# One core, attention followed by a token- and channel-mixing block: the zero tile cleared first, tail matmul pairs put together, three element-wise steps in larger pieces

## The chip, the core and the metric

The kernel runs on one core of one Trainium2 chip. A core has a matrix engine (TensorE, PE in the profile, with its weight loads shown apart as PEld), a vector engine (VectorE, DVE), a scalar engine (ScalarE, ACT), a general engine (GpSimd, POOL) and SyncE (SP), which here only issues DMAs. Each engine works through its own queue in order. An instruction may wait for semaphores that other engines or landing DMAs raise, and everything behind it on its queue then waits too. The metric is the device time of one execution in microseconds.

## The reference

The inputs are `q`, `k`, `v` of shape (8 batches, 8 heads, 576 tokens, 64), and the weights of a mixing block over 512 channels. All of it is float32.

```python
kv  = einsum('bhsd,bhse->bhde', k, v)              # 64 x 64 per head
out = einsum('bhsd,bhde->bhse', q, kv)
out = out / sqrt(mean(out*out, -1) + 1e-6) * g_norm  # per head
x   = out.transpose(0, 2, 1, 3).reshape(8, 576, 512)
a1  = alpha1 * x + beta1
u   = x + lam * einsum('ts,bsd->btd', w_tok, a1)    # token mix, 576 x 576
a2  = alpha2 * u + beta2
y   = u + lam * (relu(a2 @ w_ch1) @ w_ch2)          # channel mix, 512 -> 2048 -> 512
```

## The kernel before

**Stages.** For each of the eight batches the kernel makes the key-value products (`kv_product`, L666), the attention output with its normalisation (`qkv_groups`, L851/L858 and the steps after them), the token mix (`tok_groups`, L1020, L1029, L1053; for batch 0 `tok_first`, L1083), a transposed and scaled copy `a2t` of the mixed rows (`ut_groups`), the first channel matmul with its ReLU (`ch1_groups`, L1169 for even and L1211 for odd batches) and the second channel matmul with the final add and the store (`ch2_groups`, L1260, L1270, L1273). Matmuls of the large stages are in bf16 with a moving operand of 512 columns (320 in odd batches).

**Tokens.** A batch's 576 tokens are four chunks of 128 and a tail of 64. The tails of two batches share one tile, so odd batches carry the tails of their even neighbour. The chunks are handled in `PAIRS = ((0, 1), (2, 3), (4,))`.

**The token mix.** For a pair of chunks the mix sums over four token chunks of 128 and the tail of 64. In batches 0 and 1 (`b < MIX`) the tail is a fifth matmul per chunk. From batch 2 on the function `group` issues for each chunk four matmuls (L1020), and then for the pair two matmuls over the 64 tail rows (L1029), one on the upper and one on the lower half of the array's rows. VectorE adds the result to `x` (L1035), then scales it by `alpha2` into `a2b` (L1041), and SyncE issues DMAs that transpose `a2b` into `a2t` (L1148). In batches 0 and 1 the transposes are matmuls against an identity (L1118), evacuated by ScalarE (L1127) or VectorE (L1128). The tails of an odd batch and of its neighbour are mixed in `tails` (L1053), one on each column half of the array.

**The start.** All weights and the first batches' inputs have to be loaded. Before the first real work and in holes of the plan TensorE gets filler matmuls on a zeroed tile `wz`, which shares its memory with `a2b` (L1572; the zeroing is L1368). VectorE clears four small tiles first (L1368 to L1371). Batch 0's mix is done in halves of 256 columns (`tok_first`, adds at L1100). Batch 1's queries are split into a high and a low bf16 part (`split_q`, casts at L533 and L534, subtractions at L621) and transposed by matmuls (L644). W_ch1 comes in four pieces and is cast to bf16 (L533, L534); W_ch2 comes in four pieces and is multiplied by `lam` into bf16 in sixteen parts of 512 columns (L1493). The third part of the parameters, `beta1` (L1299), is loaded into the first of the W_ch2 buffers once its parts have been scaled, and the loads for batch 2 stand behind it on SyncE.

**The order of the work.** The kernel first records operations with their reads and writes, and then a list scheduler (`Prog.schedule`) sets the order on every queue from priorities, assumed costs per operation and the eight PSUM banks; some operations may go to one of two engines. `Prog.plan` repeats this with priorities taken from due times of the first channel matmuls, keeps the best of eight rounds, shifts priorities at random once for each of five seeds, and schedules a last time. Where TensorE would have nothing to do before the first channel matmul, the scheduler puts in a filler. So any change of an assumed cost, a piece or a seed can move instructions on all queues. Waits on semaphores come from the recorded reads and writes. `matmul_held` (L428) issues a matmul that keeps the weights of the one before.

Of the kernel before, what the change touches and what calls it, by code (L numbers as in the profile page):

```python
# [49 lines left out]
class Prog:  # L50
# [6 lines left out]
    def __init__(self, nc, stack):  # L57
# [10 lines left out]
        self.look = 0.5  # L68

# [54 lines left out]
    def plan(self, due, rounds, seeds):  # L124
# [6 lines left out]
        def run(pri):  # L131
# [8 lines left out]
            for o in movable:  # L140
                o.pri = pri[o]
            self.schedule()
# [39 lines left out]
    def schedule(self):  # L182
# [91 lines left out]
        while left:  # L274
            progressed = False
            for e, q in queues.items():
                while q and free[e] <= t + 1e-9:
# [14 lines left out]
                    if pick is None and e == "PE" and first:  # L292

                        pick = self.op("PE", 0.43 if t < 6.0 else 0.22, lambda e: self.warm[1](e, self.warm[3]),
# [139 lines left out]
def bass_transnormer_attn__then__resmlp_affine_kernel(  # L434
# [15 lines left out]
    with ExitStack() as stack:  # L450
# [146 lines left out]
        def split_q(b):  # L597
# [3 lines left out]
            if b < 2:  # L601
                parts = [(cs, hs) for hs in HALVES for cs in PAIRS]
            else:
                parts = [(cs, ALL[0]) for cs in PAIRS]
# [406 lines left out]
        def tok_groups(b):  # L1011
            def group(cs):
                n = len(cs)
                t = P.ptile(n)
                rows = rows_of(b, cs[0])
# [9 lines left out]
                if scs < 5:  # L1025
                    def g(e):
                        for i, c in enumerate(cs):
                            r = slice(64 * i, 64 * i + 64)
                            m = e.matmul(t.ap()[:, i, :], wt[r, 4 + i, 128 * c:128 * c + 128],  # L1029
                                         rtt[r, b % 2, :], start=False, stop=True)  # L1030
                        return m
                    P.op("PE", 0.28, g, r=wtk(4) + ["wt5"] + rkeys(b, 4), w=[t])
# [7 lines left out]
                for c in cs:  # L1040
                    P.op(dve_pool(512), 0, lambda e, c=c: e.tensor_tensor(  # L1041
                        out=a2b[rows, c, :], in0=xv(b, (c,)), in1=a2_bc[rows, :], op=ALU.mult),
                        r=xkeys(b, c) + ["a2"], w=[("a2b", c)], pri=-100, port=True)
            def tails():
# [18 lines left out]
                if b > 1:  # L1063
                    P.op(dve_pool(512), 0, lambda e: e.tensor_tensor(
                        out=a2b[:, 4, :], in0=x, in1=a2_bc[:], op=ALU.mult),
                        r=xk + ["a2"], w=[("a2b", 4)], pri=-100, port=True)
            for cs in PAIRS[:2]:
                yield lambda cs=cs: group(cs)
# [3 lines left out]
        def tok_first():  # L1072

            def half(a):
                hs = HALVES[a]
                lo, hi = 256 * a, 256 * a + 256
                ts = [P.ptile(1) for g in PAIRS[:2]]

                def part(sc):
                    def f(e):  # L1080
                        for cs, t in zip(PAIRS[:2], ts):
                            for i, c in enumerate(cs):
                                m = e.matmul(t.flat()[:, 256 * i:256 * i + 256],  # L1083
                                             tok_w(sc, c), rsrc(0, sc, lo, hi),
                                             start=(sc == 0 and i == 0), stop=(sc == 4),
# [519 lines left out]
```

## Time and profile before

| what | value |
|---|---|
| median of 3 runs (lowest, highest) | 364.8 us (364.39, 364.88) |
| profiled execution, its own time | 365.61 us |
| its span, first to last instruction | 363.6 us |
| TensorE busy | 357.7 us, 98% of the span |
| VectorE busy | 240.8 us, 66% |
| ScalarE busy | 160.2 us, 44% |
| GpSimd busy | 26.6 us, 7% |
| mean DMA rate | 165 GB/s |

In the profile a row of a group reads: line, engine, operation, output<-inputs, shape, count, then busy time, mean of one in ns, idle time of the engine before them and what ended it. A timeline row reads: start in us from the span's beginning, time, engine, line, operation, output<-input, shape, count. Neighbouring matmuls overlap in these times, because a matmul's end is modelled; the pace is read from start to start. A matmul in float32 shows as two rows of the count unless it is a transpose.

### The profile page before, as it was taken

To read this page: it belongs to the slowest core of one execution; us is meant where nothing else is said; L and a number is where in the kernel's file an instruction comes from. 1 tells how busy PE (TensorE), PEld (TensorE's weight loads), DVE (VectorE), ACT (ScalarE), POOL (GpSimd) and SP (SyncE) were. 2 spreads that over 40 slices of the span, in tenths; PEclk is the share of its full clock that TensorE was granted. 3 is DMA by queue.
4 is the path that set the end of the run, shared out by engine and by line. 5 is a ranking of instruction groups with operands and counts; after the bars stand their busy time and mean duration, and the time that the engine had idled before them with its cause. 6 is when DMAs were issued, how large, how long until landed. Compare 5 with 4: busy or idle time off the path is not lost.

```text
span 363.6 us, 7716 instructions
## 1 busy us (share of the span) xinstructions
PE 357.7 (98%) x3479; PEld 203.9 (56%) x3255; DVE 240.8 (66%) x366; ACT 160.2 (44%) x277; POOL 26.6 (7%) x34
## 2 busy tenths in 40 slices
PE   7999999999999999999999999999999999999996
PEld 3788555477644654457644454457654554457644
DVE  3388997995985388866984368865986368830021
ACT  1466883248740287017740188007750186007600
POOL 4046412500000000000000000000000000000000
PEclk9999999999999999999999999999999999999999
DMA  7999928999407960299637860199027410130012
GB/s 286 367 364 382 404 112 318 374 193 274 174 21 183 286 250 1 60 159 275 237 72 187 239 241 2 43 161 260 3 58 132 132 31 0 43 117 29 2 58 87
DMA packets 79896, 60.15 MB, mean 165 GB/s; under 512 B 53037, under 2 KB 63541, under 8 KB 79736
## 3 DMA queue, kind: packets, MB, share of 16 engines
q1 hardware_dynamic: 79840, 59.67, 55.3%
q8 instruction: 26, 0.43, 0.5%
q14 instruction: 6, 0.05, 0.0%
q10 hardware_dynamic: 24, 0.01, 0.0%
HBM read 38.82 MB, written 9.44 MB: 133 GB/s over the span
## 4 chain that ended last, share of the span: by engine, by line
PE 98%; DVE 0%; issue 0%
PE ps L1260 34%; PE ps L1211 19%; PE ps L1169 14%; PE ps L1020 7%; PE ps L666 5%; PE ps L1572 2%; PE ps L851 2%; PE ps L428 2%; PE ps L1053 1%; PE ps L858 1%; PE ps L1083 1%; PE ps L1118 1%; PE ps L693 1%; PE ps L1029 1%; PE ps L1241 1%; PE ps L951 1%
## 5 line engine op out<-in xcount | busy, mean ns | idle before, releaser
L1260 PE MATMUL ps<-w,ht 128*128 128x512 bf16 x560 | 125.8, 379 | 0.0
L1158 ACT ACTIVATE ht<-ps,hb 128x512 bf16<-128x512 f32 (+1 forms) x96 | 70.9, 739 | 45.7 <-PE ps L1211 35.0
L1260 PEld LDWEIGHTS ps<-w,ht 128*128 128x128 bf16 x560 | 53.3, 98 | 62.9 <-issue 1.4
L1211 PE MATMUL ps<-a2t,w 128*128 128x320 bf16 (+1 forms) x512 | 72.4, 299 | 0.0
L1211 PEld LDWEIGHTS ps<-a2t,w 128*128 128x128 bf16 x512 | 49.4, 98 | 20.5
L1169 PE MATMUL ps<-a2t,w 128*128 128x512 bf16 x240 | 55.3, 379 | 0.8 <-issue 0.8
L728 ACT ACTIVATE kvd<-ps 64x128 bf16<-64x128 f32 x24 | 6.5, 271 | 92.3 <-PE ps L666 92.2
L1270 DVE TENSOR_TENSOR xm<-ps,xm 128x512 f32<-128x512 f32 x31 | 20.8, 685 | 28.6 <-PE ps L1260 28.5
L1169 PEld LDWEIGHTS ps<-a2t,w 128*128 128x128 bf16 x240 | 22.4, 98 | 26.4 <-issue 1.3
L890 DVE TENSOR_REDUCE small<-sq 128x16 f32<-128x1024 f32 (+2 forms) x20 | 20.5, 1026 | 16.0 <-ACT sq L888 16.0
L1020 PE MATMUL ps<-rt,wt 128*128 128x512 bf16 x112 | 26.9, 380 | 0.0
L1159 ACT ACTIVATE ht<-ps 128x512 bf16<-128x512 f32 (+1 forms) x32 | 20.2, 649 | 4.0 <-PE ps L1169 1.5
L1035 DVE TENSOR_TENSOR xm<-ps,xm 128x1024 f32<-128x1024 f32 x14 | 17.1, 1221 | 5.6 <-PE ps L1029 4.9
L888 ACT ACTIVATE sq<-ps 128x1024 f32<-128x1024 f32 (+2 forms) x20 | 17.5, 873 | 6.9 <-PE ps L858 4.1
L909 DVE TENSOR_TENSOR xm<-ps,small 128x1024 f32<-128x1024 f32 (+1 forms) x18 | 19.9, 1105 | 0.5
L733 DVE TENSOR_TENSOR kvd<-ps,kvd 64x128 bf16<-64x128 f32 x24 | 6.9, 289 | 18.6 <-ACT kvd L728 18.3
L666 PEld LDWEIGHTS ps<-vf,kf 64*64 64x64 f32 x1008 | 16.0, 135 | 4.6 <-issue 4.6
L666 PE MATMUL ps<-vf,kf 64*64 64x64 f32 x1008 | 17.8, 221 | 0.0
L1020 PEld LDWEIGHTS ps<-rt,wt 128*128 128x128 bf16 x112 | 10.4, 98 | 12.8 <-issue 1.1
L1270 DVE TENSOR_TENSOR xtl<-ps,xtl 128x512 f32<-128x512 f32 x4 | 2.8, 692 | 20.2 <-PE ps L1260 20.1
L533 ACT ACTIVATE qs<-qf 128x1024 bf16<-128x1024 f32 (+1 forms) x15 | 13.8, 961 | 5.0 <-DMA qf<-in_q_dram 5.0
L1041 DVE TENSOR_TENSOR a2b<-xm,a_bc 128x512 bf16<-128x512 f32 x24 | 15.5, 687 | 0.4
(134 smaller groups left out, 358.7 us busy)
## 6 DMA issues: line engine op xcount, KB each, us to landing
out_dram<-xm SPq DMA_DIRECT2D x31, 256.0 KB, 2.8
qf<-in_q_dram SPq DMA_DIRECT2D x7, 1024.0 KB, 6.7
kf<-in_k_dram SPq DMA_DIRECT2D x6, 1152.0 KB, 7.6
vf<-in_v_dram SPq DMA_DIRECT2D x6, 1152.0 KB, 10.7
stg<-in_moe_w_ch_dram SPq DMA_DIRECT2D x3, 1024.0 KB, 12.8
kf<-in_moe_w_ch_dram SPq DMA_DIRECT2D x2, 1024.0 KB, 13.7
kf<-in_k_dram SPq DMA_DIRECT2D x2, 576.0 KB, 4.9
vf<-in_v_dram SPq DMA_DIRECT2D x2, 576.0 KB, 5.9
```

The lines of the kernel that those rows point to most:

```text
L666: m = e.matmul(t.ap(slice(64 * x, 64 * x + 64))[:, y, 0:64], nine(kf, b, a)[r, x, c, :], nine(vf, b, a)[r, x, c, :], start=(c == 0), stop= ...
L888: P.op("ACT", act_us(64 * m), lambda e: e.activation(sqv, raw(), ACT.Square), r=[t], w=[("sq", sqs)])
L890: P.op("DVE", dve_us(64 * m), lambda e: e.tensor_reduce(out=smv, in_=sqv.rearrange("p (h d) -> p h d", h=m), axis=AX.X, op=ALU.add), r=[(" ...
L909: P.op("DVE", dve_us(64 * m), lambda e: e.tensor_tensor(out=x3, in0=split(raw()), in1=inv, op=ALU.mult), r=[t, ("sm", sms)], w=xk, pri=-200)
L1020: m = e.matmul(t.ap()[:, i, :], tok_w(sc, c), rsrc(b, sc), start=(sc == 0), stop=(sc == 4))
L1035: P.op("DVE", dve_us(512 * n), lambda e: e.tensor_tensor(out=x, in0=t.ap(rows) if n > 1 else t.flat(rows), in1=x, op=ALU.add), r=[t] + xk, ...
L1158: o = P.op("ACT", act_us(n) + 0.09, lambda e: e.activation(dst, src(), ACT.Relu, bias=hb[:, fj:fj + 1]) if b > 1 else e.activation(dst, sr ...
L1159: dst, src(), ACT.Relu, bias=hb[:, fj:fj + 1]) if b > 1 else e.activation(
L1169: m = e.matmul(t.flat(), w, a2t[:, dj, 0:512], start=(dj == 0), stop=(dj == 3))
L1211: m = e.matmul(t.ap()[:, i, 0:n], w1[:, dj, 128 * fj:128 * fj + 128], a2t[:, dj, 320 * i:320 * i + n], start=(dj == 0), stop=(dj == 3))
L1260: m = e.matmul(t.flat(), ht[:, fj, 128 * c:128 * c + 128], w2[:, fj, :], start=(fj == 0), stop=(fj == 15))
L1270: P.op("DVE", dve_us(512), lambda e: e.tensor_tensor(out=x, in0=t.flat(), in1=x, op=ALU.add), r=[t] + keys, w=keys)
```

## The change

- The zero tile's clearing gets a priority ahead of everything (`self.first`) and an assumed cost of 0.3 instead of 0.2; the clearing of `eps` is set early too. The assumed cost of a filler stays that of the slow clock until 6.1 instead of 6.0.
- `split_q`: batches 0 and 1 are split over all eight heads at once, as the later batches were already.
- `tok_groups`: from batch 2 on both pairs of chunks are issued first (`all_chunks`), then the four tail matmuls of both pairs in one operation, then the adds and scalings (`finish`). The scalings into `a2b` are fixed to VectorE.
- `tok_first`: one two-bank tile and one addition of 4 x 256 columns per half, instead of two one-bank tiles with an addition of 2 x 256 each.
- `load_w`: each piece of W_ch2 is scaled in two parts of 1024 columns instead of four of 512.
- The five seeds of the plan are others.

In the order that results, fillers on TensorE go from 27 to 18 and VectorE's instructions from 366 to 356; the other TensorE instructions and the 153 DMAs that SyncE issues are the same in number, in another order.

```diff
--- before.py
+++ after.py
@@ -66,6 +66,7 @@
         self.warm = None
         self.spare = 0.0
         self.look = 0.5
+        self.first = []
 
     def ptile(self, n):
         return PTile(self, n)
@@ -139,6 +140,8 @@
             self.lastw.pop(self.warm[3], None)
             for o in movable:
                 o.pri = pri[o]
+            for o in self.first:
+                o.pri = -3000.0
             self.schedule()
             return max(o.end for o in self.ops)
 
@@ -291,7 +294,7 @@
                         break
                     if pick is None and e == "PE" and first:
 
-                        pick = self.op("PE", 0.43 if t < 6.0 else 0.22, lambda e: self.warm[1](e, self.warm[3]),
+                        pick = self.op("PE", 0.43 if t < 6.1 else 0.22, lambda e: self.warm[1](e, self.warm[3]),
                                        r=self.warm[2], w=[self.warm[3]])
                         if ready(pick, t):
                             left += 1
@@ -598,10 +601,7 @@
 
             par = b % 2
             lo_ = 64 * par
-            if b < 2:
-                parts = [(cs, hs) for hs in HALVES for cs in PAIRS]
-            else:
-                parts = [(cs, ALL[0]) for cs in PAIRS]
+            parts = [(cs, ALL[0]) for cs in PAIRS]
             for cs, hs in parts:
                 n, c0, nh = len(cs), cs[0], hs.stop - hs.start
                 rows = slice(0, 128) if c0 < 4 else slice(lo_, lo_ + 64)
@@ -1010,9 +1010,7 @@
 
         def tok_groups(b):
             def group(cs):
-                n = len(cs)
-                t = P.ptile(n)
-                rows = rows_of(b, cs[0])
+                t = P.ptile(len(cs))
                 scs = 5 if b < MIX else 4
                 for i, c in enumerate(cs):
                     def f(e, i=i, c=c):
@@ -1022,14 +1020,12 @@
                         return m
                     P.op("PE", 0.217 * scs, f,
                          r=[kk for s in range(scs) for kk in wtk(s) + rkeys(b, s)], w=[t])
-                if scs < 5:
-                    def g(e):
-                        for i, c in enumerate(cs):
-                            r = slice(64 * i, 64 * i + 64)
-                            m = e.matmul(t.ap()[:, i, :], wt[r, 4 + i, 128 * c:128 * c + 128],
-                                         rtt[r, b % 2, :], start=False, stop=True)
-                        return m
-                    P.op("PE", 0.28, g, r=wtk(4) + ["wt5"] + rkeys(b, 4), w=[t])
+                if b < MIX:
+                    finish(cs, t)
+                return t
+
+            def finish(cs, t):
+                rows, n = rows_of(b, cs[0]), len(cs)
                 x = xv(b, cs)
                 xk = [kk for c in cs for kk in xkeys(b, c)]
                 P.op("DVE", dve_us(512 * n), lambda e: e.tensor_tensor(
@@ -1038,7 +1034,7 @@
                 if b < 2:
                     return
                 for c in cs:
-                    P.op(dve_pool(512), 0, lambda e, c=c: e.tensor_tensor(
+                    P.op("DVE", dve_sb(512), lambda e, c=c: e.tensor_tensor(
                         out=a2b[rows, c, :], in0=xv(b, (c,)), in1=a2_bc[rows, :], op=ALU.mult),
                         r=xkeys(b, c) + ["a2"], w=[("a2b", c)], pri=-100, port=True)
             def tails():
@@ -1061,11 +1057,27 @@
                 P.op("DVE", dve_us(512), lambda e: e.tensor_tensor(
                     out=x, in0=t.flat(), in1=x, op=ALU.add), r=[t] + xk, w=xk, pri=-100)
                 if b > 1:
-                    P.op(dve_pool(512), 0, lambda e: e.tensor_tensor(
+                    P.op("DVE", dve_sb(512), lambda e: e.tensor_tensor(
                         out=a2b[:, 4, :], in0=x, in1=a2_bc[:], op=ALU.mult),
                         r=xk + ["a2"], w=[("a2b", 4)], pri=-100, port=True)
-            for cs in PAIRS[:2]:
-                yield lambda cs=cs: group(cs)
+            def all_chunks():
+                ts = [group(cs) for cs in PAIRS[:2]]
+
+                def g(e):
+                    for cs, t in zip(PAIRS, ts):
+                        for i, c in enumerate(cs):
+                            r = slice(64 * i, 64 * i + 64)
+                            m = e.matmul(t.ap()[:, i, :], wt[r, 4 + i, 128 * c:128 * c + 128],
+                                         rtt[r, b % 2, :], start=False, stop=True)
+                    return m
+                P.op("PE", 0.56, g, r=wtk(4) + ["wt5"] + rkeys(b, 4), w=ts)
+                for cs, t in zip(PAIRS, ts):
+                    finish(cs, t)
+            if b < MIX:
+                for cs in PAIRS[:2]:
+                    yield lambda cs=cs: group(cs)
+            else:
+                yield all_chunks
             if b % 2:
                 yield tails
 
@@ -1074,22 +1086,22 @@
             def half(a):
                 hs = HALVES[a]
                 lo, hi = 256 * a, 256 * a + 256
-                ts = [P.ptile(1) for g in PAIRS[:2]]
+                t = P.ptile(2)
+                ts = [t]
 
                 def part(sc):
                     def f(e):
-                        for cs, t in zip(PAIRS[:2], ts):
-                            for i, c in enumerate(cs):
-                                m = e.matmul(t.flat()[:, 256 * i:256 * i + 256],
-                                             tok_w(sc, c), rsrc(0, sc, lo, hi),
-                                             start=(sc == 0 and i == 0), stop=(sc == 4),
-                                             skip_group_check=True)
+                        for c in range(4):
+                            m = e.matmul(t.flat()[:, 256 * c:256 * c + 256],
+                                         tok_w(sc, c), rsrc(0, sc, lo, hi),
+                                         start=(sc == 0 and c % 2 == 0), stop=(sc == 4),
+                                         skip_group_check=True)
                         return m
                     P.op("PE", 0.44, f, r=wtk(sc) + rkeys(0, sc, hs) + ["tokh"] * a,
                          w=ts + ["tokh"] * (1 - a))
                 for sc in range(5):
                     part(sc)
-                for cs, t in zip(PAIRS[:2], ts):
+                for cs in ((0, 1, 2, 3),):
                     rows, n = rows_of(0, cs[0]), len(cs)
                     x = xv(0, cs, lo, hi)
                     xk = [kk for c in cs for kk in xkeys(0, c, hs)]
@@ -1365,8 +1377,8 @@
              w=["wst2"], dma_us=0.6)
         P.chain = False
 
-        P.op("DVE", 0.2, lambda e: e.memset(wz.bitcast(mybir.dt.uint32), 0), w=["wz"])
-        P.op("DVE", 0.2, lambda e: e.memset(eps[:], 1e-6), w=["eps"])
+        wz_op = P.op("DVE", 0.3, lambda e: e.memset(wz.bitcast(mybir.dt.uint32), 0), w=["wz"])
+        P.op("DVE", 0.2, lambda e: e.memset(eps[:], 1e-6), w=["eps"], pri=-1900)
         P.op("DVE", 0.1, lambda e: e.memset(ones[:], 1.0), w=["ones"])
         P.op("DVE", 0.4, lambda e: e.memset(kv32, 0.0), w=["kvz"])
         P.op("ACT", 1.6, lambda e: e.activation(small[:, 0, 0:1], eps[:], ACT.Sqrt),
@@ -1487,13 +1499,15 @@
                 P.op("SP", 0.6, lambda e: e.dma_start(
                     s_, moe_w_ch2[512 * n:512 * n + 512, :].rearrange(
                         "(j p) c -> p j c", p=128)), w=sk, dma_us=2.75)
-                for hh in range(4):
+                for hh in range(2):
                     if n > 1:
                         P.readers.setdefault(("w2p", n, hh), []).extend(P.readers["w2s"])
-                    P.op(dve_pool(512), 0, lambda e, hh=hh: e.tensor_tensor(
-                        out=w2[:, 4 * n + hh, :], in0=s_[:, hh], in1=lam_bc[:],
+                    P.op(dve_pool(1024), 0, lambda e, hh=hh: e.tensor_tensor(
+                        out=w2[:, 4 * n + 2 * hh:4 * n + 2 * hh + 2, :],
+                        in0=s_[:, 2 * hh:2 * hh + 2],
+                        in1=lam_bc[:, None, :].to_broadcast([128, 2, DM]),
                         op=ALU.mult), r=sk + ["lam"], w=[("w2p", n, hh)], pri=60, port=True)
-                P.lastw[("w2", n)] = [y for hh in range(4) for y in P.lastw[("w2p", n, hh)]]
+                P.lastw[("w2", n)] = [y for hh in range(2) for y in P.lastw[("w2p", n, hh)]]
 
         due = {}
 
@@ -1571,7 +1585,8 @@
         def warm(e, t):
             return e.matmul(t.flat(), wz[:, 0:128], wz, start=True, stop=True)
         P.warm = (next(iter(due)), warm, ["wz"], P.ptile(1))
-        P.plan(due, 8, (53, 59, 68, 82, 104))
+        P.first = [wz_op]
+        P.plan(due, 8, (30002, 30023, 30039, 30073, 30134))
         P.synchronize()
         P.emit()
 
```

## The prediction

> **What bounds the kernel now.** I read the page first (span, engines, granted clock, chain), then TensorE's waits, then the timeline engine by engine round each edit.
>
> ```profile
> span 363.6 us, 7716 instructions
> ...
> PE 357.7 (98%) x3479; PEld 203.9 (56%) x3255; DVE 240.8 (66%) x366; ACT 160.2 (44%) x277; POOL 26.6 (7%) x34
> ...
> PEclk9999999999999999999999999999999999999999
> ...
> PE 98%; DVE 0%; issue 0%
> ...
> PE ps L1572 <- DVE a2b L1368: 1.9, 1, 1.9
> PE ps L1169 <- issue: 0.8, 1, 0.8
> ```
>
> TensorE is busy 357.7 of 363.6 us, the chain that ended last is TensorE's own queue, and it waits twice: 1.9 us for the zero tile at the start and 0.8 us for nothing that the profile names. So an edit counts only if it takes instructions off TensorE's queue, starts that queue earlier, or makes it wait. Vector, Scalar and GpSimd work is free until TensorE reaches its result too soon. The profiled execution took 365.61 us, 2.0 more than its span and 0.8 more than the median of the runs, 364.8; the unnamed 0.8 us may be that difference. I sum against the profiled execution and carry the difference over to the median.
>
> **Part 1: the zero tile first, and fewer fillers.**
>
> ```profile
> 0.91 0.48 DVE L1371 MEMSET kvd<- 128x512 f32 x1 [0.91 <-PEq L1590]
> ...
> 1.54 0.27 DVE L1368 MEMSET a2b<- 128x256 uint32 x1
> ...
> 1.87 5.73 PE L1572 MATMUL ps<-a2b 128*128 128x512 bf16 x13 [1.87 <-DVE a2b L1368]
> 7.53 0.59 PE L1340 MATMUL ps<-xtl,ones 1*128 1x64 f32 x2
> 8.04 1.28 PE L666 MATMUL ps<-vf,kf 64*64 64x64 f32 x72
> ...
> 12.62 1.04 PE L1572 MATMUL ps<-a2b 128*128 128x512 bf16 x4
> ...
> 36.08 1.03 PE L1572 MATMUL ps<-a2b 128*128 128x512 bf16 x4
> ...
> 45.07 3.62 PE L1169 MATMUL ps<-a2t,w 128*128 128x512 bf16 x16
> ...
> 1.25 0.46 SPq L555 DMA_DIRECT2D vf<-in_v_dram  x1
> ...
> vf<-in_v_dram SPq DMA_DIRECT2D x1, 576.0 KB, 4.9
> ...
> L1572 PE MATMUL ps<-a2b 128*128 128x512 bf16 x27 | 9.6, 502 | 1.9 <-DVE a2b L1368 1.9
> ...
> 208.59 1.04 PE L1169 MATMUL ps<-a2t,w 128*128 128x512 bf16 x4 [0.81 <-issue]
> ```
>
> The rows of L1572 are the fillers, 27 by their group's row: 13 at the head and then 4, 3, 2, 1 and 4 (first and last shown). In the changed kernel's order 13+3+2 = 18 stand. The 13 at the head stay; nine later ones go, and the real work that the planner now sets in their places was in the queue anyway. A matmul of this size is issued every (3.62-1.04)/(16-4) = 0.215 us, so nine are 1.94 us.
>
> The zero tile's memset moves from fourth to first on Vector. It now starts at 0.91 and ends at 1.18; with the same 0.06 us to TensorE as now, TensorE starts at 1.24 instead of 1.87, a gain of 0.63 us. The other memsets are pushed back by 0.27 us; their first reader on TensorE's path, the broadcast of L1340, comes after 7 us. After the fillers the changed order has the first key-value product (L666) where the broadcast stood; the fillers end at 1.24+5.6 = 6.8, and its value rows landed at 1.25+4.9 = 6.15, so 0.65 us of slack remain, just enough to keep the gain. Bounds: 0 (clock, below) to 0.65.
>
> At the head a filler takes 5.73/13, about 0.43 us, twice the 0.215 of later ones: TensorE starts at half pace, though the granted clock reads 9 tenths throughout. [...]
>
> Nine fillers are worth their time only if their places are not waits. With all 27 in place TensorE has no wait between the start and the unnamed one at 208 us, and the loads it needs land first; where results are tightest (first mix, first transposes) I allow 0.2 us of new waits.
>
> **Part 2: tail pairs put together, six batches.** Now a pair of 64-row matmuls follows each half of the mix; after, one group of four follows both.
>
> ```profile
> 102.11 1.89 PE L1020 MATMUL ps<-rt,wt 128*128 128x512 bf16 x8
> 103.93 0.39 PE L1029 MATMUL ps<-rtt,wt 64*128 64x512 bf16 x2
> 104.25 1.90 PE L1020 MATMUL ps<-rt,wt 128*128 128x512 bf16 x8
> 106.08 0.39 PE L1029 MATMUL ps<-rtt,wt 64*128 64x512 bf16 x2
> 106.41 1.90 PE L1260 MATMUL ps<-w,ht 128*128 128x512 bf16 x8
> ...
> 69.33 1.05 PE L1053 MATMUL ps<-rt,wt 128*64 128x512 bf16 x8
> 70.22 0.38 PE L1053 MATMUL ps<-rtt,wt 128*64 128x512 bf16 x2
> ```
>
> Start to start, eight matmuls take 1.82 us where 8 x 0.215 = 1.72 would do, so 0.10 is lost on entering the pair; the pair holds the queue 0.32, of which 0.215 is work and 0.10 the way back. Two pairs cost 2 x 0.42 = 0.84. For two pairs back to back the nearest row is L1053, where four pairs (there on column halves) take 70.22-69.33 = 0.89, 0.22 a pair. Four together then cost 0.10+0.22+0.32 = 0.64: 0.20 saved a batch, 1.2 in six. Bounds: 0 (the switch is paid between pairs too) to 6 x 0.42 = 2.5 (all four run at once).
>
> [...]
>
> ```profile
> 106.34 5.15 SPq L1148 DMA_TRANSPOSE a2t<-a2b  x4
> ...
> 124.58 1.89 PE L1169 MATMUL ps<-a2t,w 128*128 128x512 bf16 x8
> ```
>
> The first add (1.22 us) and its scalings, all on Vector before and after, now start about 2 us later. On SyncE batch 2's four transposes of the result (L1148) stand behind four transposes of the next queries in the new order, some 5 us by the row above. Now they are issued by 111.5 and their reader L1169 starts at 124.58: 13 us of cover, of which 5 to 7 are used; without it each us would be paid. The number of DMAs stays at 153; the stores that swap places with transposes have no reader.
>
> **Part 3: what the new order exposes.**
>
> ```profile
> 75.72 0.60 PE L1118 MATMUL ps<-ident,xtl 128*128 128x128 f32 x4
> 76.34 1.97 PE L1118 MATMUL ps<-ident,xm 128*128 128x128 f32 x16
> 78.23 2.42 PE L666 MATMUL ps<-vf,kf 64*64 64x64 f32 x144
> 80.58 0.58 PE L1211 MATMUL ps<-a2t,w 128*128 128x320 bf16 x3
> ...
> 76.14 3.21 ACT L1127 ACTIVATE a2t<-ps,ab 128x128 bf16<-128x128 f32 x5 [5.46 <-PE ps L1118]
> ...
> 77.50 0.80 DVE L1128 TENSOR_SCALAR a2t<-ps,ab 128x512 bf16<-128x512 f32 x1
> ```
>
> Before batch 1's channel mixing TensorE transposes the mixed rows (L1118), then does 144 rows of key-value products, 2.4 us, then starts L1211. Those products hide the last evacuation of the transposes, which ends at 76.14+3.21 = 79.35, 1.12 us after the last transpose was issued (78.23). In the changed order both product groups stand ahead of the transposes, and L1211's counterpart follows the last transpose directly. It must wait for that evacuation: 1.1 us. Bounds: 0.8 (one evacuation of the 0.80 row) to 1.6 (two in a row on one engine). Everything on TensorE stands behind it.
>
> **Part 4: larger pieces.**
>
> ```profile
> L1493 DVE TENSOR_TENSOR w<-stg,lam_bc 128x512 bf16<-128x512 f32 x11 | 7.8, 778 | 0.0
> L915 DVE TENSOR_TENSOR rt<-xm,e1g_bc 128x1024 bf16<-128x1024 f32 x2 | 2.4, 1224 | 0.1
> L621 POOL TENSOR_TENSOR qs<-qf,qs 128x512 bf16<-128x512 f32 x3 | 3.5, 1178 | 0.8 <-ACT qs L533 0.6
> L1100 DVE TENSOR_TENSOR xm<-ps,xm 128x512 f32<-128x512 f32 x4 | 2.6, 686 | 0.6 <-PE ps L1083 0.6
> ...
> SPq L1299 <- DVE w L1493: 10.8, 1, 10.8
> ...
> 40.88 1.67 DVE L795 COPY kvd<-kvd 64x256 bf16<-64x256 bf16 x3
> 41.15 1.32 POOL L1493 TENSOR_TENSOR w<-stg,lam_bc 128x512 bf16<-128x512 f32 x1 [2.08 <-DMA stg<-in_moe_w_ch_dram]
> ```
>
> A scaling of W_ch2 of twice the size costs 1.22 (the L915 row's shape) against 2 x 0.68 to 2 x 0.78: 0.1 to 0.3 us each off Vector, seven there now. The mix addition of batch 0 becomes two of 1.22 instead of four of 0.686. Off TensorE's path both are worth nothing; they are covered by the first channel mixing, and if that cover went, the first W_ch2 matmul would wait by what is late. SyncE now waits 10.8 us for a late scaling before the loads of batch 2; in the new order the first two scalings free that buffer, so those loads start some 8 us sooner: no wait ends there, but it keeps the earlier TensorE from running into them. Batch 1's q subtraction on GpSimd becomes one piece of about 2 x 1.18 = 2.4 us. While GpSimd ran 1.32 us, three Vector copies took 1.67 us; alone the last of them takes 0.22. A longer GpSimd piece can hold Vector's weight copies back: 0 to 2.4 us, taken as 0 because those copies have work between them and their reader.
>
> **The sum.** -0.63 - 1.94 - 1.2 + 1.1 + 0.2 = -2.5 us: the profiled execution would go from 365.6 to 363.1, the median from 364.8 to 362.3 us.
>
> **The rivals.**
> - *The clock follows its own time.* If full pace still comes at about 7.5, the products that start at 6.8 run at half pace for 0.7 us and more, losing 0.35 to 0.6: 362.8. For it: the doubled fillers. Against: nothing that I see. It stays faster.
> - *The front has no slack for nine fillers.* GpSimd's 2.4 us piece holds Vector's copies of W_ch1, or the tight first mix is late, and TensorE waits 1 to 2.4 us: 363.1 to 364.5, centre 364.0. For it: the 1.67 row. Against: no wait in the front today. In this case the planner's fillers were real waiting, and the change hardly does what it says.
> - *Slower: four PSUM banks held.* The four tails need both two-bank tiles of the mix at once, half of the eight banks, and the first is freed only after the second's matmuls and an add of 1.22. If the W_ch2 matmuls behind want such a bank, TensorE waits up to 0.2+1.22 = 1.4 us a batch, 8.4 in six: 362.3+8.4 = 370.7. It decides from 2.5/6 = 0.42 us a batch. Against: the matmuls behind need one bank at a time, and four others are there.
>
> **How the numbers follow.** Forecast 0.64, its own range 361.0 to 363.5 (the tails at 2.5 or 0, which is 1.3 and 1.2 off the 1.2 taken; the exposed evacuation's 0.8 to 1.6 lies within). Clock 0.14. No slack 0.13, of it 0.04 faster. Banks 0.09. A measurement of this kernel tells about 0.2% (0.7 us) from no change: faster 0.64+0.14+0.04 = 0.82, same 0.09, slower 0.09. The range reaches from 361.0 to 364.2 and leaves out the banks and the end of the no-slack case.
>
> **What would show it.** Right: TensorE's first row at 1.2; 18 fillers; four-matmul groups holding the queue about 0.55 us, six times; one new wait of about 1.1 us before batch 1's first channel matmul, ended by Scalar or Vector; no others. Wrong: waits of TensorE before 60 us on Vector's weight copies; a wait after each mix; products near 7 us at twice their 1.28.

## The result and the profile after

The changed kernel takes 361.71 us (median of 5 runs, 360.87 to 362.39), the kernel before 364.39 us beside it (median of 5, 363.34 to 364.88): a ratio of 0.993 with a 95% interval of 0.9902 to 0.9959, 2.7 us less. The profiled execution took 360.87 us with a span of 359.1, the fastest of its five; the one of before, 365.61, was at the slow end of its kernel, which took 363.11 to 365.86 in the runs beside the experiments. So the two profiles lie 4.7 us apart where the medians lie 2.7 apart, and a part of what they show is chance.

From the page of the changed kernel (span, and busy time of each engine):

```profile
span 359.1 us, 7676 instructions
...
PE 353.5 (98%) x3470; PEld 202.7 (56%) x3246; DVE 239.7 (67%) x356; ACT 158.3 (44%) x274; POOL 25.9 (7%) x31
```

Its waits, TensorE's two and one of SyncE's queue (engine, line, what it waited for: us in total, times, longest):

```profile
PE ps L1586 <- DVE eps L1381: 1.2, 1, 1.2
PE ps L1223 <- DVE a2t L1140: 1.0, 1, 1.0
...
SPq L1311 <- DVE w L1505: 3.5, 1, 3.5
```

TensorE has lost 4.2 us of work and still bounds the span. Its start wait is 1.2 instead of 1.9, the unnamed 0.8 is gone, and one new wait of 1.0 stands before batch 1's first channel matmul (L1223, the counterpart of L1211). SyncE's wait for a scaling of W_ch2 has fallen from 10.8 to 3.5 us; the profile shows nothing on TensorE's path that hung on it.

The timeline of the changed kernel, TensorE first, then in a second block VectorE and ScalarE (start, length in us, engine, line, what it writes and reads, count, and the idle time ahead with what ended it):

```profile
1.19 4.77 PE L1586 MATMUL ps<-a2b 128*128 128x512 bf16 x13 [1.19 <-DVE eps L1381]
6.03 1.28 PE L666 MATMUL ps<-vf,kf 64*64 64x64 f32 x72
7.23 1.12 PE L1352 MATMUL ps<-xm,ones 1*128 1x512 f32 x2
...
11.13 0.82 PE L1586 MATMUL ps<-a2b 128*128 128x512 bf16 x3
...
33.22 0.60 PE L1586 MATMUL ps<-a2b 128*128 128x512 bf16 x2
...
72.51 2.33 PE L666 MATMUL ps<-vf,kf 64*64 64x64 f32 x144
...
76.79 0.38 PE L1130 MATMUL ps<-ident,xtl 128*128 128x128 f32 x2
78.22 2.34 PE L1223 MATMUL ps<-a2t,w 128*128 128x320 bf16 x16 [1.05 <-DVE a2t L1140]
...
103.36 0.61 PE L1070 MATMUL ps<-rtt,wt 64*128 64x512 bf16 x4
103.90 4.27 PE L1272 MATMUL ps<-w,ht 128*128 128x512 bf16 x19
```

```profile
0.86 0.27 DVE L1380 MEMSET a2b<- 128x256 uint32 x1 [0.86 <-PEq L1605]
...
76.55 1.53 DVE L1140 TENSOR_SCALAR a2t<-ps,ab 128x512 bf16<-128x512 f32 x2
...
75.57 2.33 ACT L1139 ACTIVATE a2t<-ps,ab 128x128 bf16<-128x128 f32 x5
```

The zero tile is cleared at 0.86 to 1.13 and TensorE starts at 1.19. There are 13+3+2 = 18 fillers. The four tails hold the queue for 103.90-103.36 = 0.54 us. Both product groups (72.51) stand ahead of the transposes, and the channel matmul behind them waits for Vector's last evacuation, which ends at 76.55+1.53 = 78.08.

**Where the 4.5 us between the two spans went**, cut at the same work in both:

| stretch of TensorE's queue | before | after | difference |
|---|---|---|---|
| start of the span to the first fillers | 1.87 | 1.19 | -0.68 |
| fillers and L1340's two short broadcasts at the head (in the changed kernel the broadcasts stand later, at 10.77, and hold the queue 11.13-10.77 = 0.36) | 8.04-1.87 = 6.17 | 6.03-1.19+0.36 = 5.20 | -0.97 |
| first product to batch 1's first channel matmul | 80.58-8.04 = 72.54 | 78.22-6.03-0.36 = 71.83 | -0.71 |
| from there to the end | 363.6-80.58 = 283.02 | 359.1-78.22 = 280.88 | -2.14 |

The third row holds nine fillers less (-1.94) and the new wait: it takes 78.22-76.79 = 1.43 from the last transposes where two would hold the queue 0.22, so +1.21; 0.02 is left over. The fourth row is the tails (-1.2) and a stall that only the kernel before has: its group of L1169 took 1.84 us for four matmuls (206.75 to 208.59), 0.97 too long. The second row is no part of any step: the half pace at the head ended sooner in that execution (the full clock's record begins at 4.85 us, in the profile of before at 7.88).

### The profile page after: what moved, and what is told of

It is laid out like the page before. It is cut to its first block, busy times and chain, and to the rows that moved or that the text cites. A ratio compares the mean times of both kernels' runs of the same rounds, so it can differ in the third digit from the quotient of the medians.

```text
span 359.1 us, 7676 instructions
## 1 busy us (share of the span) xinstructions
PE 353.5 (98%) x3470; PEld 202.7 (56%) x3246; DVE 239.7 (67%) x356; ACT 158.3 (44%) x274; POOL 25.9 (7%) x31
## 4 chain that ended last, share of the span: by engine, by line
PE 97%; DMA 1%; DVE 1%; SPq 0%; issue 0%
PE ps L1272 34%; PE ps L1223 20%; PE ps L1181 15%; PE ps L1018 7%; PE ps L666 5%; PE ps L851 2%; PE ps L431 2%; PE ps L858 1%; PE ps L1049 1%; DMA vf<-in_v_dram 1%; PE ps L1095 1%; PE ps L693 1%; PE ps L1253 1%; PE ps L1130 1%; PE ps L1070 1%; PE ps L951 1%
## 5 line engine op out<-in xcount | busy, mean ns | idle before, releaser
L1223 PE MATMUL ps<-a2t,w 128*128 128x320 bf16 (+1 forms) x512 | 72.6, 299 | 1.0 <-DVE a2t L1140 1.0
L1223 PEld LDWEIGHTS ps<-a2t,w 128*128 128x128 bf16 x512 | 49.4, 98 | 21.8 <-ACT a2t L1139 1.3
L1181 PE MATMUL ps<-a2t,w 128*128 128x512 bf16 x240 | 54.5, 379 | 0.0
L1018 PE MATMUL ps<-rt,wt 128*128 128x512 bf16 x112 | 25.8, 379 | 0.0
L733 DVE TENSOR_TENSOR kvd<-ps,kvd 64x128 bf16<-64x128 f32 x24 | 6.9, 288 | 18.3 <-ACT kvd L728 18.1
L621 DVE TENSOR_TENSOR qs<-qf,qs 128x1024 bf16<-128x1024 f32 x13 | 16.5, 1297 | 0.3 <-ACT qs L536 0.3
```

The lines of the kernel that those rows point to most:

```text
L1018: m = e.matmul(t.ap()[:, i, :], tok_w(sc, c), rsrc(b, sc), start=(sc == 0), stop=(sc == 4))
L1181: m = e.matmul(t.flat(), w, a2t[:, dj, 0:512], start=(dj == 0), stop=(dj == 3))
L1223: m = e.matmul(t.ap()[:, i, 0:n], w1[:, dj, 128 * fj:128 * fj + 128], a2t[:, dj, 320 * i:320 * i + n], start=(dj == 0), stop=(dj == 3))
```

## The experiments

The kernel before ran beside each of them; ratios are to those runs, with 95% intervals. Some of these traces lack single matmul records, which shows as many "issue" waits of 0.2 us with a group of 7 where 8 were issued; they are no waits.

**1. The zero tile first, alone** (kernel before, otherwise in its own order):

```diff
+        P.sequence.remove(wz_op)
+        P.sequence.insert(0, wz_op)
         P.synchronize()
```

> The kernel before, with the zero tile's clearing as Vector's first instruction and nothing else moved: 27 fillers, the old order. Mine (TensorE's queue is the time): TensorE starts 0.6 us sooner (1.2 instead of 1.87) and everything behind it follows, 364.4 to 363.8 us; the first key-value product, at 8.04 in the profile of before, comes at about 7.4. Rival (full pace has its own time): the fillers start sooner but end no sooner, the product stays near 8.0, 364.4. Second rival: the start is gained and given back in the first 25 us, where the distances from a result to its reader on TensorE are about half a microsecond; the timeline would show TensorE waiting there.

Measured: 364.4 us (363.6 to 364.86), ratio 0.9995 [0.9983, 1.0007]: nothing that can be told from no change. Its profile has the gain at the head and a loss at 207 us (timeline of TensorE):

```profile
1.19 5.28 PE L1572 MATMUL ps<-a2b 128*128 128x512 bf16 x13 [1.19 <-DVE a2b L1368]
...
205.30 1.03 PE L1169 MATMUL ps<-a2t,w 128*128 128x512 bf16 x4
207.83 1.04 PE L1169 MATMUL ps<-a2t,w 128*128 128x512 bf16 x4 [1.50 <-issue]
```

TensorE starts 0.68 us sooner, and the unnamed wait of before, in the middle of the same eight matmuls, is 1.5 us instead of 0.8. At 205.30 the work is 1.45 us ahead of the kernel before, at 207.83 only 0.76, so 0.7 of the lead is lost in this stall, and none in the front, where the second rival would have it. A wait that grows when the work comes sooner looks like something that arrives at its own time.

**2. Without the later fillers** (kernel before, 13 at the head kept, 14 dropped):

```diff
+        fill = sorted((o for o in P.sequence if P.warm[3] in o.tiles), key=lambda o: o.start)
+        out_ = set(fill[13:])
+        P.sequence[:] = [o for o in P.sequence if o not in out_]
```

> The kernel before without its 14 fillers behind the 13 at the head (4, 3, 2, 1 and 4), all other instructions in the old order: the fillers' results are used by nothing, so no part of the computation is left out. Theory A (the fillers only lengthen the queue, the results behind them are ready): 14 x 0.215 = 3.0 us less, 361.4 us, and no new wait. Theory B (the fillers stand in holes that are there anyway): TensorE waits where they stood, for Scalar and Vector, 364.4 us unchanged; then the nine fillers that the changed kernel saves are holes that its new order closed. By the distances in the profile of before (0.4 to 0.9 us from a result to its reader at these places) I expect something between: about 1.5 us less, 362.9, with short waits at 13, 35 and 37 us.

Measured: 362.92 us (362.41 to 363.77), ratio 0.9952 [0.9937, 0.9968], 1.6 us of the 3.0 us that 14 fillers hold. Its waits of TensorE name what the fillers had covered:

```profile
PE ps L1118 <- DVE xm L1100: 0.5, 1, 0.5
...
PE ps L858 <- ACT qt L533: 0.4, 1, 0.4
PE ps L1402 <- DMA ht<-in_moe_w_tok_dram: 0.3, 1, 0.3
```

The first is the first transposes behind batch 0's mix. From the first product to the second group of L1184 it takes 41.04-7.77 = 33.27 us, before 42.83-8.04 = 34.79: 1.52 less. The unnamed wait near 207 us is not in this profile either, so a part of the total may be that wait's. A filler that goes is worth its 0.215 us only as far as the results behind it are ready.

**3. The tails joined, alone** (the changed `tok_groups` in the kernel before):

> The kernel before with the joined tail pairs alone (27 fillers, old pieces, old seeds). Mine: 0.2 us less in each of six batches, 1.2 us in all, 363.2; each group of four tails holds TensorE's queue for 0.54 us behind 0.10 of entry. [...] Rival 2 (held PSUM banks): a wait after each mix, at worst 8 us, 364.4 to 372.

Measured: 363.83 us (363.24 to 364.89), ratio 0.9977 [0.9965, 0.9989], 0.8 us by the ratio. The unnamed wait stands in this profile too, and longer: 1.3 us where before has 0.8. The tails' own price could not be read off the total until that wait was out of the way (experiment 8).

**4. The products behind the transposes** (changed kernel; the second product group of batch 2, with its evacuation and the loads that wait for it, moved behind batch 1's transposes):

```diff
+        late = [o for o in P.sequence if o in P.kv2]
+        ...
+        P.sequence[:] = ([o for o in rest[:at] if o not in held] + late + held + rest[at:])
```

> The changed kernel with one move: the second group of key-value products of batch 2 (36 instructions, 72 rows, 1.05 us), its evacuation on Scalar and Vector and the loads that wait for it stand behind the transposes of batch 1's mixed rows, not ahead of them. Mine (the new wait of 1.05 us, 1.2 in starts, is uncovered evacuation): the wait falls to about 0.1 to 0.2, 361.7 to 360.7 us. Rival: the products' own evacuation, now late, stops batch 2's attention matmuls instead (they start 2.2 us after the channel matmuls do), and the wait moves there, 361.7.

Measured: 361.24 us (360.94 to 361.31, 4 runs), ratio 0.9904 [0.9890, 0.9918], against 0.9930 [0.9902, 0.9959] for the changed kernel. The intervals overlap, so the total alone does not settle it; the timeline does:

```profile
76.20 0.38 PE L1135 MATMUL ps<-ident,xtl 128*128 128x128 f32 x2
76.51 1.28 PE L667 MATMUL ps<-vf,kf 64*64 64x64 f32 x72
78.14 2.34 PE L1230 MATMUL ps<-a2t,w 128*128 128x320 bf16 x16 [0.35 <-DVE a2t L1145]
```

With 72 rows of products between the transposes and the channel matmul the wait falls from 1.0 to 0.4, less far than expected. The cause of the new wait is the order, as predicted. That the move gains time is not shown: from the first product to batch 1's first channel matmul it takes 78.14-5.96 = 72.18 us, and 78.22-6.03 = 72.19 in the changed kernel, since small new waits stand ahead of it, among them 0.2 us before the transposes, for Vector's addition (L1035 in this kernel).

**5. The five later fillers of the changed kernel dropped** (same edit as in 2):

> The changed kernel without its five later fillers (three at 11.1 us and two at 33.2 us in its profile); the order of everything else is the same. If a filler holds the queue and hides no wait, five of them are 5 x 0.216 = 1.08 us: about 360.6 us against 361.7. Rival: in the kernel before without its 14 later fillers (362.9 us) about half of their 3.0 us came back as waits in front of 36 us; the same share here leaves 0.5 us, about 361.2. If more than 1 us comes back, the five places were waits and the time stays at 361.7.

Measured: 362.18 us (361.68 to 362.53), ratio 0.9935 [0.9918, 0.9951]: 1.08 us of work gone and nothing gained. That is the third case named ahead, that more than 1 us comes back, but part of it comes back where no filler stood. The timeline has an unnamed wait at a new place, in the middle of batch 1's transposes:

```profile
75.12 0.38 PE L1130 MATMUL ps<-ident,xm 128*128 128x128 f32 x2
76.53 0.88 PE L1130 MATMUL ps<-ident,xm 128*128 128x128 f32 x6 [1.03 <-issue]
```

**6. Every filler as two halves** (kernel before; same columns, 54 instructions more):

```diff
-            return e.matmul(t.flat(), wz[:, 0:128], wz, start=True, stop=True)
+            e.matmul(t.flat()[:, 0:256], wz[:, 0:128], wz[:, 0:256], start=True, stop=False, ...)
+            return e.matmul(t.flat()[:, 256:512], wz[:, 0:128], wz[:, 256:512], start=False, ...)
```

> The kernel before with each of its 27 fillers issued as two matmuls of 256 columns: the same columns, so the same TensorE time to within 0.1 us, but 27 matmuls and 27 weight loads more in the instruction stream ahead of the unnamed wait near 207 us. Theory: that wait is TensorE running out of instructions; it sits at a fixed count of instructions and must move 54 instructions towards the start, out of the second group of L1169 into the products of L666 before it, and change its length with it (0.8 us now; up to 3 us if the fetch comes at its old time of 206.2 us, about 1 us if the fetch moves along): the time is 364 to 367 us. Rival: the wait belongs to those matmuls, their operands or their bank; it stays in the second group of L1169 at 0.8 us, and the time is 364.5.

Measured: 364.23 us (362.94 to 365.79), ratio 0.9990 [0.9974, 1.0007]. The wait did not move by 54 instructions as the theory had it: it is gone. The eight matmuls stand together:

```profile
206.16 1.89 PE L1169 MATMUL ps<-a2t,w 128*128 128x512 bf16 x8
207.88 0.19 PE L851 MATMUL ps<-kvd,qt 128*128 128x64 bf16 x1
```

That rules out the rival, that the wait belongs to those matmuls or their operands: they are untouched; the count of instructions ahead of them changed, and they come 0.6 us sooner. What the wait is, the records of the instruction queue (q8 on the page: 26 transfers, all of 16,384 bytes, one for about every 252 recorded TensorE instructions: from the first to the last of them (6558-261)/25 in the kernel before) tell:

| kernel | transfer ran | TensorE went on at | after landing | too long by |
|---|---|---|---|---|
| before | 206.22 to 207.21 | 208.59 | 1.38 | 0.97 |
| 1, zero tile first | 205.50 to 206.47 | 207.83 | 1.36 | 1.67 |
| 3, tails joined | 205.68 to 206.64 | 207.91 | 1.27 | 1.47 |
| 4, products behind | 203.69 to 204.66 | 206.10 | 1.44 | 0.47 |
| 5, no later fillers | 73.70 to 75.10 | 76.53 | 1.43 | 1.19 |
| 5, no later fillers | 205.02 to 205.99 | 207.21 | 1.22 | 0.42 |
| after | 203.04 to 203.93 | no stall | | 0 |
| 6, fillers halved | 199.00 to 200.25 | no stall | | 0 |

In all six stalls such a transfer has landed 1.22 to 1.44 us before TensorE goes on; in the last two rows, where the transfer came earlier, there is no stall. So the reading is that TensorE had run out of instructions.

Counting bears it out. In the traces that lack no record (the kernel before, experiments 7 and 10), the instruction with which TensorE goes on after such a stall has 449, 1729 or 4289 recorded TensorE instructions (matmuls, weight loads, semaphore instructions) ahead of it. 1729 is 449 + 5 x 256 and 4289 is 449 + 15 x 256, and the transfers that landed just before are the first, the sixth and the sixteenth. The changed kernel reaches counts 1729 and 4289 1.29 and 1.76 us after their transfers landed and does not stall; it escapes narrowly. Both kernels of experiment 8 reach count 4289 about 4 us after.

By these counts one transfer goes with 256 recorded instructions, a block in what follows. What decides when a transfer starts stays open: it began 3 matmuls ahead of the end of the block in experiment 1 and 6 ahead in the kernel before.

**7. Later fillers dropped, counts kept** (experiment 5, with five of the thirteen head fillers halved, so that every later instruction keeps the count it has in the changed kernel):

> The changed kernel without its five later fillers, as before (362.2 us, with a new unnamed wait of 1.0 us among batch 1's transposes at 75 us and one of 0.3 at 207), and with five of the thirteen fillers at the head issued as two matmuls of 256 columns, so that every later instruction has the same count of instructions before it as in the changed kernel (361.7 us). Theory: the two unnamed waits are TensorE waiting for its next block of instructions, whose ends lie at fixed counts; with the counts of the changed kernel, which shows no such wait, they are gone, and the five fillers are worth their 1.1 us: about 360.6 us. Rival: the fillers were covering something at those places; the waits stay and the time is 362.2 us.

Measured: 361.53 us (361.23 to 362.03), ratio 0.9927 [0.9912, 0.9942]. Half a hit: the waits at 75 and 207 us have shrunk to about 0.2 us each by start-to-start times and are no longer listed, as the theory says, and the time is still not 360.6. Its waits of TensorE:

```profile
PE ps L1589 <- DVE eps L1381: 1.2, 1, 1.2
PE ps L1223 <- DVE a2t L1140: 1.0, 1, 1.0
PE ps L693 <- issue: 0.3, 1, 0.3
```

From the first product (6.84 us here) to batch 1's first channel matmul (79.09) it takes 72.25 us, the changed kernel 78.22-6.03 = 72.19. The five fillers' 1.08 us came back: by start-to-start times 0.50 at 15.3 us, where an instruction transfer landed at 14.32 and TensorE went on at 15.82; 0.31 at 36.4 us; 0.21 at 75.8 us, where the sixth transfer had landed at 74.36; the rest in smaller pieces. So 0.7 us of it is again waiting for instructions. With such stalls taken out, the stretch takes 72.25-0.50-0.21 = 71.54 us here and (79.12-6.48)-1.19 = 71.45 in experiment 5, against 72.19: the places of the five fillers are worth about 0.7 of their 1.08 us, and the stalls hide it.

**8. The zero tile first, and the tails joined, each with the fillers halved** (experiments 1 and 3 on top of 6):

> The kernel before with every filler issued as two halves (364.2 us, and no unnamed wait in its profile) and the zero tile cleared first on Vector. With the instruction blocks out of the way the earlier start should come through: 0.6 us less, 363.6, with no unnamed wait above 0.3 us. Rival: the start comes 0.7 us earlier but the clock rises at its own time or the front waits for loads, so that nothing is left: 364.2 us.

> The kernel before with every filler issued as two halves (364.2 us) and the tails of each later token mix put together. Mine: 0.20 us in each of six batches, 363.0 us, with no unnamed wait above 0.3 us. Rival: the pair's switch is paid inside the group too, so that the tails give 0.6 us or less: 363.6 us or more. The 0.7 us that they gave without the split had an unnamed wait of 1.3 us in the profile.

Measured: zero tile first 363.08 us (362.61 to 365.49), ratio 0.9982 [0.9964, 1.0000]; tails joined 363.1 us (361.8 to 363.76), ratio 0.9966 [0.9949, 0.9984]; the halved fillers by themselves 0.9990. No unnamed wait in either profile. The zero tile gives 0.0008 x 364 = 0.3 us by the ratios and 1.0 by the medians of the spans (361.8 to 360.85), the tails 0.9 by the ratios and 1.0 by the spans (361.8 to 360.8). These two ran in another session than 6, in which the kernel before was 0.5 us shorter too (spans of 362.4 and 361.9), so 0.5 of each 1.0 may be the session's. The tails agree with the forecast; the sign of the zero tile does, its size is not settled. In its profile a wait of 0.4 us for a landing stands behind the head fillers, which the half pace, ending early there (1.19+2.65 = 3.84 us), no longer covers:

```profile
5.84 0.43 PE L1340 MATMUL ps<-xtl,ones 1*128 1x64 f32 x2 [0.37 <-DMA xtl<-in_g_norm_dram]
6.21 1.28 PE L666 MATMUL ps<-vf,kf 64*64 64x64 f32 x72
```

The tails are seen in the timeline of the kernel with joined tails: mix, tails and next matmul at 101.75, 105.30 and 105.83 us, 4.08 us against 106.41-102.11 = 4.30 before.

```profile
101.75 3.62 PE L1018 MATMUL ps<-rt,wt 128*128 128x512 bf16 x16
105.30 0.60 PE L1070 MATMUL ps<-rtt,wt 64*128 64x512 bf16 x4
105.83 2.33 PE L1272 MATMUL ps<-w,ht 128*128 128x512 bf16 x10
```

**9. The larger pieces undone** (changed kernel, same order, each larger piece issued as two halves at its place):

> The changed kernel with the same order, but each larger piece issued as two halves at its place: the eight scalings of W_ch2, the two mix additions of batch 0, and batch 1's q copies and subtractions. My theory prices the larger pieces at nothing: within 0.3 us of 361.7. Rival: the longer Vector and GpSimd work holds the front back (0.15 to 0.3 us more for each of six scalings on Vector, 0.15 for each addition of batch 0): 1 us or more slower, with new waits of TensorE on Vector before 60 us. The other way, if the long GpSimd piece was holding Vector's copies back, it is faster by 0.3 us or more.

Measured: 361.89 us (361.6 to 363.15), ratio 0.9933 [0.9915, 0.9951]: the changed kernel's time to 0.2 us. In this order the size of the pieces is worth nothing that can be told.

**10. The changed kernel with the seeds of before** (`(53, 59, 68, 82, 104)`):

> The changed kernel with the five seeds of the kernel before: the order is then another one, with 26 fillers instead of 18 (13, 4, 4, 1 and 4). If fewer fillers are what the seeds give, eight more cost up to 8 x 0.216 = 1.7 us: 363.4 us. Rival: the fillers stand where TensorE would wait anyway, and the rest of the change brings the time: 361.7 to 362.3 us.

Measured: 370.57 us (369.61 to 371.64), ratio 1.0176 [1.0155, 1.0197]. Both theories missed by 7 us or more; the fillers have little to do with it. TensorE's waits and Vector's timeline:

```profile
PE ps L1018 <- DVE kvd L733: 4.6, 1, 4.6
PE ps L1130 <- DVE xm L1031: 1.2, 1, 1.2
...
PE ps L1181 <- issue: 0.9, 1, 0.9
```

```profile
70.73 4.39 DVE L621 TENSOR_TENSOR qs<-qf,qs 128x1024 bf16<-128x1024 f32 x2
75.04 0.67 DVE L621 TENSOR_TENSOR qs<-qft,qs 64x512 bf16<-64x512 f32 x1
```

In this order three subtractions of batch 2's queries, 5.0 us on Vector (70.73 to 75.7), stand ahead of the evacuation of the products (L733), and batch 1's mix waits for what that evacuation frees. Of the 8.9 us to the changed kernel two waits have 5.8, and the unnamed one at 0.9 is back (a transfer landed at 213.29, and TensorE went on at 214.58).

A third part is no wait. The page's row of the granted clock has a dip in its ninth slice, and TensorE's timeline shows doubled spacing there:

```profile
PEclk9999999989999999999999999999999999999999
...
78.53 1.91 PE L1018 MATMUL ps<-rt,wt 128*128 128x512 bf16 x4
80.23 0.63 PE L1018 MATMUL ps<-rtt,wt 128*128 128x512 bf16 x1
```

Four matmuls take (80.23-78.53)/4 = 0.43 us each instead of 0.215. The trace's clock records have half the clock from 77.39 to 80.80 us, just behind the wait of 4.6 us; 3.41 us at half pace cost about 1.7 us (an estimate from these two numbers). No other trace here has such a stretch between its head and its end.

**11. Experiments 4 and 5 together:**

> The changed kernel with both edits: the second product group of batch 2 behind batch 1's transposes (0.9904 of the kernel before by itself, against 0.993) and no later fillers. If the two add up, 0.9 us and 0.5 to 1.1 us go off 361.7: 359.7 to 360.3 us. Rival: without the fillers the front runs into results that are not there, and the products that were moved have less cover: no better than the move alone, 361.1.

Measured: 360.92 us (360.81 to 361.4), ratio 0.9905 [0.9888, 0.9921]. By the totals the two do not add up; the time is that of the move alone (0.9904), as the rival said. The profiles say less: from the first product to batch 1's first channel matmul it takes 77.97-6.40 = 71.57 us, 0.61 less than with the move alone (72.18), while the half pace at the head, which differs from execution to execution, lasted to 5.88 us instead of 4.25. The intervals of the totals reach 0.6 us either way, so they cannot tell this. The move is the only edit that points below the changed kernel's 0.9930, and the intervals of the two overlap.

## Why the prediction was right

362.3 us was forecast, 361.0 to 364.2 as the range, and 361.71 came. The sum was -2.5 us, the medians moved by 364.39-361.71 = 2.7. Of the 0.6 us between forecast and result 0.4 is the kernel before, whose median was 364.8 in the three runs of the forecast; and 0.24 of the 2.7 lies outside the span (last section), where the sum had nothing. Term by term:

- **The start, -0.63.** The first row came at 1.19 and the gain was 0.68. The 0.65 us of slack behind it was used up in the profiled execution, because the fillers ended sooner than the 6.8 of the forecast: the value rows landed at 5.98, the chain of the page runs over that landing, and TensorE was idle 0.1 us for it before the product at 6.03 (0.3 in experiment 4). What was not foreseen is that alone, in the old order, the same step gave 0.2 us by the ratio, with an interval that includes no change; in its profile the stall at 207 us had grown from 0.97 to 1.67, by as much as the start had gained.
- **Thirteen fillers at 5.6 us.** They took 6.03-1.19 = 4.84 in the profiled execution, and 4.1 to 5.65 in the others that start at 1.19. Kernels with the same head differ that much, so in a single profile this term is mostly chance.
- **Nine fillers, -1.94.** The third row of the table has it, with the wait, to 0.02. It is the term that stood nearest to failing: dropping 14 in the old order gave 1.6 of 3.0 us, and dropping five more from the new one gave nothing by the total, about 0.7 of 1.08 with the stalls for instructions taken out.
- **The tails, -1.2.** The timeline has 0.54 for four on the queue and 4.08 against 4.30 for a whole mix, 0.22 a batch where 0.20 was taken. By the totals 0.8 us with the stall and 0.9 without.
- **The exposed evacuation, +1.1.** It is 1.21 by start-to-start times, 1.05 by the wait's own row, at the predicted place, ended by Vector where Scalar was named as likely. Experiment 4 shows that the order is the cause.
- **The front, +0.2; the larger pieces, 0.** The front's left-over is 0.02, and experiment 9 shows the pieces at 0. GpSimd's q subtraction took 2.13 us where 2.4 was worked out, with no Vector copy held back.

What the sum lacked: the unnamed 0.8 us of before. The prediction took it for the difference between the profiled execution and the median, carried it through on both sides, and so counted nothing for its end. It was a stall for instructions, and it is not in the changed kernel's profile: 0.97 us of the 4.5 between the two profiles. How often it strikes in the other executions is not shown; experiment 6, which takes it away, gives 0.4 us by the ratio with an interval that includes no change as well. So the profiles bear the sum out term by term, and the one omission can only have helped the total, by a size that stays open. That it helped was luck: the changed kernel reaches two of the counts at which others stalled 1.29 and 1.76 us after the landing (experiment 6), just late enough.

Of the rivals, *four banks held* and *no slack in the front* did not come: no wait follows a mix, and behind the start none above 0.1 us stands before 60 us. *The clock follows its own time* did not come in the changed kernel, where the products at 6.03 took their usual 1.28. In the profile of experiment 9, with the same head, it came in small: the half pace lasted to 7.12, into the products at 6.84.

## What to carry to other kernels

When the engine that bounds a kernel waits for nothing that the profile names, look for its instruction transfers: here the place hung on how many instructions stand ahead (449, 1729 or 4289), and 54 instructions more for the same columns took a stall of 0.97 us out of the profile (experiment 6). A long wait cost more than its own length here: 3.41 us at half the clock followed one of 4.6 us (experiment 10). Price a step in the order in which it will run: the same code in another order cost 9 us here (experiment 10), and a start gained by 0.68 us lost 0.7 in a stall elsewhere (experiment 1). Fillers were worth their length here only up to the next result that was late: dropping 14, 3.0 us long, gave 1.6 us (experiment 2).

## What the hardware showed that was not expected

- A late block of 16,384 bytes of instructions held TensorE for 0.2 to 1.7 us here, and it went on 1.22 to 1.50 us after the transfer landed. In the traces that lack no record such stalls stand only at counts that lie multiples of 256 recorded instructions apart (449, 1729 and 4289).
- The half pace at the head differs from run to run. In every trace the first clock record, full clock, begins where the pace doubles: at 4.85 us in the changed kernel's profile and at 7.88 in that of before. Ahead of it there is no record, and the page's row of the granted clock shows 9 tenths all the same. From the first filler on, the half pace lasted 2.65 us (experiment 8, zero tile first) to 5.93 (experiment 9) in the nine profiles that start at 1.19, and 4.96 (experiment 6) to 6.02 (the kernel before) in the five that start at 1.87; whether an earlier start shortens it is not shown by these.
- A long wait was followed by half the clock: 3.41 us of it, behind 4.6 us of waiting in experiment 10.
- The time outside the span fell by 0.24 us: 2.03 (medians) in the kernel before and its variants in experiments 1 to 3, 1.79 in the changed kernel and its variants. No run tells why.
